# Lower weight parts from an accumulating transfer instead of GpSimd subtractions, in an attention, dense-layer and expert kernel on one core

## The chip, the core and the metric

The kernel runs on one core of a Trainium2 chip. A core has five engines with a queue each, which run side by side: TensorE (PE; its weight loads are listed as PEld), VectorE (DVE), ScalarE (ACT), GpSimd (POOL) and SyncE (SP), which issues transfers. Sixteen DMA engines do the transfers of all queues. The metric is the device time of one execution in microseconds.

## What is computed

```python
def _moe2_ref(x, w_gate, w1, w2):            # after attention and a dense layer
    logits = x @ w_gate                      # 2304 tokens, 8 experts
    order = np.argsort(-logits.flatten())    # greedy: best pair of token and expert first
    ...                                      # an expert takes at most cap = 288 tokens
    for e in range(E):
        mask = assigned == e
        h = np.maximum(x[mask] @ w1[e], 0.0)
        out[mask] = h @ w2[e]
```

Ahead of it, a linear-feature attention and `(x @ w_a) * (x @ w_b) @ w_out` produce x. The result is float32; the kernel reaches that by splitting every operand of a product into an upper part (rounded to the type `F32R`) and a lower part (the rest), and adding three products: upper by upper, upper by lower, lower by upper.

## The kernel before

The program has three stages. Attention and the dense layer run until about 673 us (`Attention`, `Bilinear`). Then a router (`Router`) assigns tokens to experts in seven rounds: in each, VectorE compares and sums small tables, TensorE counts over partitions with many small products, and the two wait for one another. When the first expert is full, its tokens are known and `Experts` starts on it while the router goes on; so router and experts share the engines until about 975 us, and the last experts run alone.

An expert is eight chunks of 128 hidden features. For a chunk, `weights` (L920) gets one tile `raw` of 128 x 1024 float32 (512 KB: 512 columns of w1, 512 of w2), which SyncE loads from HBM (L917), and makes the upper part `wh` and the lower part `wl`. TensorE then does 12 products into `pa` (4 blocks by 3 passes: wh by xl, wh by xh, wl by xh), ScalarE and VectorE make the two parts `hh` and `hl` of the positive part, and 12 more products with the second half of wh and wl add into `po`. The `po` products of a chunk come after the `pa` products of the next one. Around an expert's end, `turn` transposes the next expert's gathered tokens (xg to xh and xl), and `turn_back` transposes results, which GpSimd scatters to the output (`out<-ob`, L902).

What sets the order:
- TensorE's order is written out by hand: `program` interleaves the steps of `Experts.products` with the router's phases by a table of estimated costs. TensorE never reorders, so a late operand stops all that is behind it.
- The other engines' order is set by a scheduler from the dependencies. Each queue runs in order too.
- `raw`, `wh` and `wl` have four buffers each (two pools of two, used in turn). The parts of a chunk can be made once the `po` products of the chunk four before have run; a load can start once the last reader of that `raw` is done.
- GpSimd's queue holds the subtractions of `wl`, the gathers `xg<-yd` (L881) and the scatters, in one order; an expert has three gathers and three scatters, each of 96 rows of 512 float32 (192 KB).

Before the change ScalarE writes `wh` as a rounded copy of `raw` (L924), and GpSimd subtracts it from `raw` in four pieces of 256 columns (L927).

Of the kernel before, what the change touches and what calls it, by code (L numbers as in the profile page):

```python
# [17 lines left out]
AF = mybir.ActivationFunctionType  # L18
OP = mybir.AluOpType
# [43 lines left out]
EARLY = 3  # L63
CUT = 2
SLOTS = 1
PIECE = 256
CNT, AT, ASSIGN, NEXT, TOKENS, COLUMNS, CANDS = 0.4, 0.05, 0.85, 5.6, 4.25, 2.35, 2.1
EAGER = 5
THR16, THR32, SEEN, POP = 0.7, 1.05, 0.12, 1
# [3 lines left out]
def f32(ap):  # L73
    return ap.bitcast(F32)
# [795 lines left out]
class Experts:  # L870
# [47 lines left out]
        return w, raw  # L918

    def weights(self, f):  # L920
        w, raw = self.raws.pop(0) if self.raws else self.load(f)
        wh, wl = [w.tile([128, 1024], F32R, name=n) for n in ("wh", "wl")]

        self.nc.scalar.copy(wh, raw)  # L924
        for c in range(0, 1024, PIECE):
            here = slice(c, c + PIECE)
            self.nc.gpsimd.tensor_tensor(wl[:, here], raw[:, here], f32(wh[:, here]), OP.subtract)  # L927
        return wh, wl

    def outputs(self, i):  # L930
# [273 lines left out]
```

## Time and profile before

| what | us |
|---|---|
| median of three runs | 1062.22 (1055.92 to 1063.88) |
| the profiled execution | 1050.81 |
| its span, first to last instruction | 1049.0 |
| TensorE busy | 966.7 (92%) |
| VectorE busy | 708.2 (68%) |
| ScalarE busy | 380.4 (36%) |
| GpSimd busy | 384.5 (37%) |
| GpSimd subtractions L927, 256 | 182.5 |

Matmuls are pipelined, so a busy TensorE is not one at its peak. The granted clock is a share of 2.4 GHz; 0.5 is 1.2 GHz. Waits are inferred from semaphores: a wait for several is put down to the one that came last. Instructions that issue transfers from SyncE are not counted as busy. "Line" and "L" give the line of the kernel before; behind the edit the lines of the changed kernel are lower by one or two.

### The profile page before, as it was taken

How to read it: one execution, taken by the hardware profiler on the slowest of the kernel's cores; microseconds unless marked ns; L12 is line 12 of the kernel's file. 1: busy time of each engine (PE TensorE's matmuls, PEld its weight loads, DVE VectorE, ACT ScalarE, POOL GpSimd, SP SyncE). 2: the span in 40 equal slices, each digit the busy share in tenths (PEclk: the TensorE clock that was granted, in tenths of full speed). 3: DMA queues.
4: the chain of work that ended last, by engine and by line, in shares of the span. 5: the costliest groups of instructions: out<-in, count | busy, mean ns of one | idle time of the engine just before them, and what ended most of it. 6: DMA issues, size and time to landing. Idle time of an engine off the chain costs nothing.

```text
span 1049.0 us, 18392 instructions
## 1 busy us (share of the span) xinstructions
PE 966.7 (92%) x6683; PEld 895.3 (85%) x6683; DVE 708.2 (68%) x2044; ACT 380.4 (36%) x769; POOL 384.5 (37%) x450
## 2 busy tenths in 40 slices
PE   6868898999999999999999999979987989897996
PEld 5867788989989999999999997768887978887996
DVE  7899999779887656854588886555647474665110
ACT  5755555433333333332211321122423323232452
POOL 3346565323311211210000000155656556556784
PEclk8889999999999999999999999967999989898999
DMA  8366676555443434432722331243243333334451
GB/s 269 109 186 188 209 245 190 217 166 161 141 148 122 134 111 138 122 99 83 268 81 81 111 120 62 81 134 124 75 146 113 117 108 104 121 107 126 131 164 39
DMA packets 66939, 142.98 MB, mean 136 GB/s; under 512 B 6944, under 2 KB 31648, under 8 KB 66720
## 3 DMA queue, kind: packets, MB, share of 16 engines
q1 hardware_dynamic: 63776, 132.36, 39.5%
q0 software_dynamic: 3072, 9.44, 3.1%
q8 instruction: 53, 0.87, 0.3%
q14 instruction: 38, 0.31, 0.1%
HBM read 118.96 MB, written 22.81 MB: 135 GB/s over the span
## 4 chain that ended last, share of the span: by engine, by line
PE 58%; DVE 9%; POOL 2%; issue 2%; DMA 1%; ACT 0%; POOLq 0%; SPq 0%; ACTq 0%; DVEq 0%
PE ab L81 19%; PE pa L81 10%; PE y L81 10%; PE po L81 8%; PE count L690 3%; PE count L823 2%; PE pa L254 2%; POOL wl L927 1%; PE kv L224 1%; PE pa L889 1%; DVE gone L756 1%; DVE pos L793 1%; PE count L688 1%; PE pa L235 1%; DVE scr L497 1%
## 5 line engine op out<-in xcount | busy, mean ns | idle before, releaser
L927 POOL TENSOR_TENSOR wl<-raw,wh 128x256 fp32r<-128x256 f32 x256 | 182.5, 743 | 283.0 <-DMA raw<-in_w 192.5
L81 PE MATMUL ab<-xl,w_hi 128*128 128x384 f32 x576 | 203.8, 354 | 1.5 <-DVE xl L93 1.5
L81 PE MATMUL ab<-xh,w_hi 128*128 128x384 f32 x576 | 195.5, 339 | 0.0
L81 PE MATMUL ab<-xh,w_lo 128*128 128x384 f32 x576 | 195.3, 339 | 0.0
L81 PE MATMUL y<-wo,gh 128*128 128x512 f32 x372 | 119.1, 401 | 1.5 <-ACT gh L92 1.5
L81 PEld LDWEIGHTS ab<-xl,w_hi 128*128 128x128 f32 x576 | 109.4, 190 | 4.6 <-DVE xl L93 1.9
L81 PEld LDWEIGHTS ab<-xh,w_hi 128*128 128x128 f32 x576 | 109.4, 190 | 1.8
L81 PEld LDWEIGHTS ab<-xh,w_lo 128*128 128x128 f32 x576 | 109.0, 189 | 0.0
L924 ACT CAST wh<-raw 128x1024 fp32r<-128x1024 f32 x64 | 67.2, 1050 | 112.0 <-PE po L81 88.6
L81 PE MATMUL pa<-xl,wh 128*128 128x288 f32 x256 | 84.2, 329 | 16.6 <-DVE hl L1001 8.6
L93 POOL TENSOR_TENSOR lo<-raw,hi 128x384 fp32r<-128x384 f32 (+4 forms) x46 | 49.3, 1071 | 126.0 <-ACT hi L92 126.0
L497 DVE SCALAR_TENSOR_TENSOR scr<-ybs,wg 128x512 bf16<-128x512 f32 x120 | 88.4, 737 | 4.3 <-ACT ybs L493 2.4
L81 PE MATMUL pa<-xh,wh 128*128 128x288 f32 x256 | 82.9, 324 | 0.0
L81 PE MATMUL pa<-xh,wl 128*128 128x288 f32 x256 | 82.4, 322 | 0.0
L81 PE MATMUL po<-hh,wl 128*128 128x288 f32 x256 | 81.6, 319 | 0.0
L81 PE MATMUL po<-hh,wh 128*128 128x288 f32 x256 | 80.8, 316 | 0.0
L81 PE MATMUL po<-hl,wh 128*128 128x288 f32 x256 | 80.4, 314 | 0.0
L163 POOL TENSOR_TENSOR tn<-tn 128x384 f32<-128x384 f32 (+4 forms) x43 | 40.1, 932 | 105.2 <-DMA tn<-in_qn 50.4
L81 PEld LDWEIGHTS y<-wo,gh 128*128 128x128 f32 x372 | 65.5, 188 | 9.9 <-issue 1.9
L81 PE MATMUL y<-wo,gl 128*128 128x512 f32 x186 | 73.0, 393 | 0.0
L1000 ACT ACTIVATE hh<-pa 128x288 fp32r<-128x288 f32 x64 | 26.3, 411 | 118.3 <-PE pa L81 116.5
L81 PEld LDWEIGHTS pa<-xl,wh 128*128 128x128 f32 x256 | 52.8, 206 | 18.6 <-DVE hl L1001 13.6
(246 smaller groups left out, 2184.6 us busy)
## 6 DMA issues: line engine op xcount, KB each, us to landing
raw<-in_w SPq DMA_DIRECT2D x64, 512.0 KB, 3.6
wo<-sd SPq DMA_DIRECT2D x38, 512.0 KB, 3.3
wg<-in_wab SPq DMA_DIRECT2D x22, 512.0 KB, 4.0
sd<-wo SPq DMA_DIRECT2D x12, 512.0 KB, 2.9
va<-in_va SPq DMA_DIRECT2D x16, 325.0 KB, 4.1
ybs<-in_wout SPq DMA_DIRECT2D x10, 512.0 KB, 3.9
yd<-ybs SPq DMA_DIRECT2D x18, 256.0 KB, 2.7
xraw<-xd SPq DMA_DIRECT2D x20, 192.0 KB, 2.9
```

The lines of the kernel that those rows point to most:

```text
L81: nc.tensor.matmul(out, lhs[l], rhs[r], start=first and i == 0, stop=last and i == 2)
L93: lo_engine.tensor_tensor(lo, src, f32(hi), OP.subtract)
L163: nc.gpsimd.tensor_tensor(tn, tn, tn, OP.mult)
L224: nc.tensor.matmul(kv[:, j], f[:, j], vals[b, p][:, vt, j], start=(ends[0] and k == 0 and j == 0), stop=(ends[1] and k == len(todo) - 1 an ...
L235: nc.tensor.transpose(pt[:, c:c + 128], ph[:, k, j], self.ident)
L254: nc.tensor.matmul(nv[:, i, j], qt[:, j], self.kvs[b, p][:, j], start=True, stop=True)
L497: self.nc.vector.scalar_tensor_tensor(self.scr, rows, 1.0, self.wg[:, e], op0=OP.mult, op1=OP.mult, accum_out=total)
L690: nc.tensor.matmul(cnt, cmp[:, c], oh[:, :, c], start=False, stop=(c == NT - 1))
L823: nc.tensor.matmul(got[:CH, :2 * NCH], slot[:, :, c], ids2[:, c].rearrange("p i j -> p (i j)"), start=(c == 0), stop=(c == NT - 1))
L924: self.nc.scalar.copy(wh, raw)
L927: self.nc.gpsimd.tensor_tensor(wl[:, here], raw[:, here], f32(wh[:, here]), OP.subtract)
L1000: nc.scalar.activation(hh, ps[:, :CAP], AF.Relu)
```

## The change

```diff
-PIECE = 256
...
     def weights(self, f):
         w, raw = self.raws.pop(0) if self.raws else self.load(f)
         wh, wl = [w.tile([128, 1024], F32R, name=n) for n in ("wh", "wl")]
-
+        self.nc.scalar.activation(wl, raw, AF.Copy, scale=-1.0)
+        self.nc.gpsimd.dma_start(wl, raw, accum_op=OP.add)
         self.nc.scalar.copy(wh, raw)
-        for c in range(0, 1024, PIECE):
-            here = slice(c, c + PIECE)
-            self.nc.gpsimd.tensor_tensor(wl[:, here], raw[:, here], f32(wh[:, here]), OP.subtract)
         return wh, wl
```

ScalarE now first writes the negated rounded copy into `wl`. A transfer that GpSimd's queue issues then adds `raw` to `wl` in place: raw minus its upper part is the lower part. Then ScalarE writes `wh` as before. `wl` is whole at once when the transfer has landed, where it came in four pieces. The order on TensorE and on SyncE is the same as before.

GpSimd's queue at the start of the experts and through the second one, before (wl is the lower part, xg a gather of tokens, out a scatter of results):

```order
L927 TENSOR_TENSOR wl<-raw,wh 128x256 x4
L881 DMA xg<-yd,ids 96x512 x3
L927 TENSOR_TENSOR wl<-raw,wh 128x256 x28
L881 DMA xg<-yd,ids 96x512 x3
L927 TENSOR_TENSOR wl<-raw,wh 128x256 x19
L902 DMA out<-ob,ids 2304x512
```

And the same place in the changed kernel:

```order
L925 DMA wl<-raw 128x1024
L880 DMA xg<-yd,ids 96x512 x3
L925 DMA wl<-raw 128x1024 x7
L880 DMA xg<-yd,ids 96x512 x3
L925 DMA wl<-raw 128x1024 x5
L901 DMA out<-ob,ids 2304x512
```

Four subtractions of a chunk have become one transfer at the same place of the queue.

ScalarE's queue where an expert ends and the next one's tokens are turned, before (wh is the upper part of a chunk, xh that of the tokens, ot a result, hh the upper part of a hidden block):

```order
L924 CAST wh<-raw 128x1024
L891 CAST xh_11074<-pa 128x288
L891 CAST xh_11107<-pa 128x288
L956 COPY ot_11211<-po_10470 128x288
L891 CAST xh_11126<-pa 128x288
L956 COPY ot_11213<-po_10471 128x288
L891 CAST xh_11138<-pa 128x288
L956 COPY ot_11215<-po_10472 128x288
L956 COPY ot_11217<-po_10473 128x288
L924 CAST wh<-raw 128x1024
L1000 ACTIVATE hh<-pa 128x288 x2
```

And the same place in the changed kernel:

```order
L924 ACTIVATE wl<-raw 128x1024
L890 CAST xh_10994<-pa 128x288
L890 CAST xh_11027<-pa 128x288
L955 COPY ot_11129<-po_10404 128x288
L926 CAST wh<-raw 128x1024
L890 CAST xh_11046<-pa 128x288
L890 CAST xh_11058<-pa 128x288
L955 COPY ot_11131<-po_10405 128x288
L955 COPY ot_11133<-po_10406 128x288
L955 COPY ot_11135<-po_10407 128x288
L924 ACTIVATE wl<-raw 128x1024
L926 CAST wh<-raw 128x1024
```

The negation stands where the copy wh stood, and the copy has moved down between the second and the third xh.

## Rows read from the trace of the kernel before

**Rows 1.** Stretches: from, to, length, busy us and instructions per engine, clock, DMA share, GB/s.

```profile
693.00:975.00 282.00, 253.82 (x2213) 234.19 (x2212) 160.65 (x599) 87.61 (x150) 165.25 (x220) 0.90 0.37 112
975.00:1040.00 65.00, 63.51 (x484) 62.69 (x484) 11.55 (x26) 32.43 (x59) 50.34 (x70) 1.00 0.40 122
```

**Rows 2.** TensorE's waits, 690 to 975 us: total us, times, longest us.

```profile
PE pa L81 <- DVE hl L1001: 8.6, 3, 4.6
PE pa L81 <- DVE total L795: 7.5, 2, 3.8
PE count L823 <- DVE ids L814: 7.1, 3, 4.0
PE count L803 <- DVE total L795: 1.8, 1, 1.8
```

**Rows 3.** Timeline around 806 to 811 us: start, duration, engine, line, instruction, idle before.

```profile
806.77 2.83 POOL L927 TENSOR_TENSOR wl<-raw,wh 128x256 fp32r<-128x256 f32 x4
806.90 2.73 DVE L756 TENSOR_TENSOR gone<-gone,new 128x18 f32<-128x18 f32 x1
...
811.06 0.40 PE L81 MATMUL pa<-xl,wh 128*128 128x288 f32 x1 [4.65 <-DVE hl L1001]
```

**Rows 4.** Three VectorE lines of the router: shortest/median/longest ns.

```profile
L756 DVE TENSOR_TENSOR gone<-gone,new x7: 170/706/2740, 672.7 to 942.6; 128x18 f32<-128x18 f32 x7
...
L725 DVE TENSOR_SCALAR over<-best,at x7: 235/776/786, 668.3 to 937.6; 128x18 bf16<-128x18 f32 x7
...
L755 DVE TENSOR_REDUCE new<-run x7: 396/414/424, 672.3 to 942.2; 128x18 f32<-128x144 bf16 x7
```

**Rows 5.** The page's costliest groups: count, busy us, mean ns, idle before.

```profile
L927 POOL TENSOR_TENSOR wl<-raw,wh 128x256 fp32r<-128x256 f32 x256 | 182.5, 743 | 283.0 <-DMA raw<-in_w 192.5
...
L924 ACT CAST wh<-raw 128x1024 fp32r<-128x1024 f32 x64 | 67.2, 1050 | 112.0 <-PE po L81 88.6
```

**Rows 6.** Stretches behind six stalls: the two ends of the clock, and the sum.

```profile
811.06:815.00 3.94, 3.94 (x18) 3.79 (x19) 3.84 (x16) 0.41 (x1) 0.38 (x1) 0.58 0.69 215
...
955.70:958.40 2.70, 2.70 (x12) 2.65 (x13) 0.31 (x2) 0.01 (x1) 1.74 (x2) 0.50 0.16 30
...
sum 26.05, PE 26.05 PEld 25.41 DVE 18.13 ACT 1.84 POOL 9.76; mean PE 4.34 PEld 4.24 DVE 3.02 ACT 0.31 POOL 1.63
```

**Rows 7.** Timeline around 753 us: VectorE beside a scatter that GpSimd issues.

```profile
753.00 0.78 DVE L725 TENSOR_SCALAR over<-best,at 128x18 bf16<-128x18 f32 x1
...
753.82 0.31 DVE L727 TENSOR_TENSOR gq<-oh,over 128x288 bf16<-128x288 bf16 x1
753.90 1.04 POOL L902 DMA_INDIRECT out<-ob,ids  x1 [0.16 <-issue]
...
754.16 0.45 DVE L731 TENSOR_REDUCE rows<-gq 128x16 bf16<-128x288 bf16 x1
```

**Rows 8.** Timeline at an expert boundary: TensorE's wait before a transposition.

```profile
788.11 0.44 PE L889 MATMUL pa<-ident,xg 96*128 96x96 f32 x3 [0.72 <-DVE xl L892]
```

**Rows 9.** Transfers: KB each and us to landing; stretches with one load, and one scatter.

```profile
raw<-in_w SPq DMA_DIRECT2D x64, 512.0 KB, 3.6
...
wg<-in_wgate SPq DMA_DIRECT2D x1, 2048.0 KB, 7.4
...
xg<-yd,ids POOLq DMA_INDIRECT x24, 3.1
...
994.40:996.75 2.35, 2.35 (x21) 2.34 (x20) 0.43 (x1) 1.19 (x2) 2.17 (x4) 1.00 0.71 223
...
997.10:998.10 1.00, 1.00 (x10) 1.00 (x9) 0.12 (x1) 0.41 (x1) 1.00 (x3) 1.00 0.67 197
```

**Rows 10.** Timeline: a chunk's cast on ScalarE and TensorE's first product with its wl.

```profile
780.51 1.05 ACT L924 CAST wh<-raw 128x1024 fp32r<-128x1024 f32 x1 [2.11 <-PE po L81]
...
792.85 0.29 PE L81 MATMUL pa<-xh,wl 128*128 128x288 f32 x1
...
995.56 1.05 ACT L924 CAST wh<-raw 128x1024 fp32r<-128x1024 f32 x1 [1.23 <-PE po L81]
...
1002.95 0.29 PE L81 MATMUL pa<-xh,wl 128*128 128x288 f32 x1
...
1027.95 1.05 ACT L924 CAST wh<-raw 128x1024 fp32r<-128x1024 f32 x1 [1.22 <-PE po L81]
```

## Prediction

> **What bounds the kernel now.** I start with the busy time by stretch, since the change touches only the last third. Up to 673 us the program runs attention and the dense layer, where no line of the diff runs. From 693 to 975 us the router and the experts share the engines, and from 975 to 1040 us the last experts run alone [rows 1]. In the second stretch TensorE is busy 253.8 of 282 us at a mean clock of 0.90; in the third 63.5 of 65 at 1.00. So the tail is TensorE's own work, and the stretch with the router has two leaks: 28 us of idle time and a clock that falls.
>
> The waits of TensorE say who ends the idle time: hl (8.6 us), total (7.5 and 1.8) and ids (7.1), 25.0 us together, all of them VectorE results [rows 2]. No wait for a weight chunk stands among them. The timeline shows why VectorE is late. At 806.90 us the sum gone, 128x18, takes 2.73 us; its quickest run takes 0.17 [rows 3, 4]. At 806.77 GpSimd had begun four subtractions that take 2.83 us together, and the sum ends with them. TensorE then stands still for 4.65 us until hl, which is queued behind gone on VectorE, arrives at 811.06 [rows 3]. It is not that instruction alone: over, with a minimum of 235 ns, has a median of 776, about one subtraction (743 ns) longer [rows 4, 5]. A reduction in the same chain, new, stays between 396 and 424 ns throughout [rows 4]. So certain VectorE instructions wait for GpSimd's subtractions. The reader is to see that GpSimd's 182.5 us [rows 5] are not on TensorE's path as work, but as a brake on VectorE.
>
> After each long stall the clock is at the lower of its two levels, 1.2 GHz. I took the six stretches behind the stalls of over 2.5 us (behind the last two stalls, from after the count products), up to where the clock is back: 26.05 us in all, with a granted clock between 0.50 and 0.58 [rows 6].
>
> **The change, part by part.** TensorE's order and SyncE's stay as they are.
>
> Removed: 256 subtractions, 182.5 us of GpSimd. Worth nothing on GpSimd itself; it frees VectorE. The longest stalls follow stretched instructions: gone alone gives 2.73 - 0.17 = 2.56 of the 4.65 us, and the rest comes in steps of about half a microsecond like that of over, of which the same round has several. I take all 25.0 us of [rows 2]. With the stalls goes the low clock behind them: 26.05 us at about 0.52 would be some 13.5 us at full clock, so 12.5 us saved. Term: **-37.5 us**.
>
> Does an issue of a transfer brake VectorE as a subtraction does? At 753.90 GpSimd issues a scatter for 1.04 us; under it gq takes 0.31 us and the reduction rows 0.45, while over, which ran under subtractions just before, took 0.78 [rows 7]. So no. The Trainium skill (SBUF — State Buffer, "Who interferes with whom") puts it so: a VectorE instruction with two SBUF inputs contends with a GpSimd instruction that reads SBUF. The same page ("SBUF: two separate sides") warns that VectorE's two-port modes keep GpSimd from writing descriptors; by that the issues would be late by the length of such an instruction. The scatter in these rows took 1.04 us beside VectorE; by the page's warning the issues would be later, which is one way into the same-time rival.
>
> Added on ScalarE: 64 negations of 128x1024. The copy of that shape takes 1050 ns [rows 5], so 67 us. ScalarE is busy 32.4 of 65 us in the tail [rows 1]; 17 more leave a quarter free, so it hides behind TensorE. Two consequences do not hide by themselves. The transfer starts 1.05 us after the buffers are free: below. And at each expert boundary the copy wh now stands between the second and the third xh on ScalarE. TensorE already waits there (0.72 us at 788.11, on xl, which follows xh) [rows 8]. Up to 1.05 us more at seven boundaries would be 7; I take **+5 us**.
>
> Added on GpSimd's queue: 64 accumulating transfers of 512 KB. No row of before has one. Its time on the sixteen DMA engines, X, decides, so I bound it by the nearest rows. A plain load of 512 KB keeps the engines busy 0.71 of 2.35 us = 1.67 us, start-up included [rows 9]. Without start-up: 2048 KB land in 7.4 us and 512 KB in 3.6, so 1536 KB more cost 3.8 us, or 1.27 us for 512 KB [rows 9]. The transfer must fetch two operands, raw and wl, and write one. Bounds: one pass at 1.27 us below; three passes one after the other at 1.67 = 5.0 above. I take two at the streaming price, **X = 2.54 us**, as both operands lie in SBUF and only the fetching doubles. The Trainium skill (Collectives: The Full Stack, "The bandwidth ceiling: the fold count and why AG ≠ RS ≠ AR") says that an adding transfer runs at about half the rate of a copy because it reads two sources on one ring. That speaks against the change, compared with one pass: by one pass the tail term below is nothing, by two it is 8 us. No row of before shows an adding transfer.
>
> Latency: a gather of 192 KB lands 3.1 us after issue [rows 9]; minus its bytes (192 KB at 404 KB per us, 0.5) plus 2.54 gives 5.2 us, and with the negation 6.3, or 8.0 when one load is ahead of it. What is there to cover it? A chunk's buffers come free four chunks ahead: the cast at 780.51 fills what TensorE first needs, as wl, at 792.85, so 12.3 us; in the tail 995.56 to 1002.95, 7.4 us [rows 10]. With the router running the transfer is hidden with 4 to 6 us to spare; without this cover each chunk would pay what is beyond it. In the tail it is about even.
>
> Throughput: per chunk a load 1.67, the accumulate 2.54, and three gathers and three scatters an expert, 6 x 0.67 / 8 = 0.50 [rows 9], 4.71 us in all. In the tail the casts from 995.56 to 1027.95 are nine chunks apart, 3.60 us each [rows 10]; 61 us of tail at that pace are 17 of the 64 chunks, so 47 lie in the stretch with the router. There TensorE would need (282 - 32.5) / 47 = 5.3 us a chunk: the DMA engines keep up. In the last 12 loads they don't: 12 x (4.71 - 3.60) = 13.3 us, less some 5 us of lead from the stretch before. Term: **+8 us**.
>
> Sum: -37.5 + 5 + 8 = -24.5 us. The profiled execution took 1050.81 us (span 1049.0 and 1.8 around it), 11.4 below the median of the runs, 1062.22, and below all three. Counted from its own time the sum gives 1026; the runs are judged by their median, so I give 1062.2 - 24.5 = **1038 us**.
>
> **Rivals.**
> One pass. The accumulate costs what a copy costs, X = 1.27, and the tail stays at 3.60 us a chunk: 1062.2 - 32.5 = 1030. For it: nothing in the rows but the lower bound.
> Same time. Two passes at the load's own price, X = 3.34. With the router: 47 x (5.51 - 5.3) = 10 us; tail: 12 x (5.51 - 3.60) - 5 = 18. The gain of 32.5 shrinks to about 5: 1057. Late issues would work the same way. For it: 1.67 is what a load was seen to take; against: a part of that is start-up at the memory, and this transfer reads SBUF.
> Slower: the DMA engines become the bound of all experts. One mechanism, one price: X above 3.4 us, where 47 x (2.17 + X - 5.3) + 12 x (2.17 + X - 3.60) - 5 exceeds 32.5. Three passes at 1.27 (3.8 us) give 1085, at 1.67 (5.0 us) 1155. TensorE would then wait for wl in every chunk. For it: no row shows the adding path at speed. Against: the engines are only 0.37 to 0.40 busy now [rows 1].
>
> **How the numbers follow.** Forecast 0.42, one pass 0.15, same time 0.18, slower 0.25. A measurement of this kernel tells about 1% (10.6 us) from no change. Faster by more: forecast, one pass and a little of the third case, 0.60; within 1%: 0.15; slower: 0.25. The range reaches from a little under the one-pass time, 1022, to the mildest of the slower case, 1085; left out are the dearer transfers, about 0.2. The likeliest case alone: 1030 to 1050.
>
> **What would show it.** The median of gone at 0.18 us and of over at 0.24, no stall of TensorE over 2 us between 693 and 975 us, and a mean clock there near 0.97. In the tail chunks of 4 to 4.7 us with waits of TensorE on wl. A DMA share of about 0.85 with the router running; if it is at 0.95 and TensorE waits for wl from the first expert on, X is over 3.4 and the forecast is wrong. If gone is still slow, the brake was something else.

## Result and profile after

The changed kernel takes 1031.7 us (1028.1 to 1035.1, four runs) against 1059.6 for the kernel before on the same chip: a ratio of 0.9735, with a 95% interval from 0.9677 to 0.9793. A second measurement, beside the experiments, gave 0.9774 [0.9740, 0.9807]. The forecast was 1038 in a range from 1022 to 1085, faster with 0.60; 1031.7 lies in that range. The profiled execution has a span of 1026.3 us, 22.7 less than that of before.

To compare kernels I cut every trace at four instants that all of them have: the start of `hl` of the first chunk (number 0), the start of `hl` of chunk 47 (the router ends there), the end of the last `po` product, and the end. Between the first two, router and experts share the engines; between the second and third the last experts run alone. TensorE executes the same products in each stretch in every kernel.

The stretches of the kernel before, cut so: from, to, length, then busy us and instructions of PE, PEld, DVE, ACT and POOL, the granted clock, the DMA share, GB/s.

```profile
698.75:978.54 279.79, 251.87 (x2198) 232.96 (x2199) 158.71 (x592) 87.86 (x148) 163.55 (x217) 0.91 0.36 111
978.54:1039.09 60.55, 59.14 (x455) 58.60 (x453) 11.34 (x25) 30.46 (x55) 47.28 (x66) 1.00 0.41 124
1039.09:1049.00 9.91, 1.80 (x12) 1.01 (x10) 0.00 (x0) 2.08 (x5) 2.75 (x3) 0.74 0.21 60
```

The same three stretches of the changed kernel:

```profile
700.68:944.52 243.84, 242.82 (x2199) 225.38 (x2200) 122.55 (x591) 130.11 (x194) 77.08 (x82) 0.95 0.94 227
944.52:1013.93 69.41, 61.39 (x455) 58.78 (x453) 11.32 (x25) 42.95 (x69) 18.09 (x21) 1.00 0.93 229
1013.93:1026.30 12.37, 1.80 (x12) 1.01 (x10) 0.00 (x0) 2.08 (x5) 2.85 (x3) 0.73 0.17 49
```

The first stretch is 35.95 us shorter. TensorE's idle time in it fell from 27.9 us (279.79 - 251.87) to 1.0, and its busy time by 9.05 for the same products, as the clock rose from 0.91 to 0.95. VectorE needs 122.55 us in place of 158.71 for the same 591 or 592 instructions: 36.2 us of VectorE's busy time had been brake, not work. The second stretch is 8.86 us longer: TensorE does the same 455 matrix instructions and stands idle 8.0 us where it stood 1.4. The end is 2.5 us longer, and the first stretch starts 1.9 us later. Together -35.95 + 8.86 + 2.46 + 1.93 = -22.7.

TensorE's waits in the two stretches of the changed kernel (total us, times, longest; the first row is of the tail, the other two of the stretch with the router), which answer to [rows 2]:

```profile
PE pa L80 <- DMA wl<-raw: 6.8, 7, 1.7
...
PE pa L80 <- DVE xl L891: 0.6, 3, 0.2
PE pa L888 <- DVE xl L891: 0.3, 1, 0.3
```

The waits for hl, total and ids have gone. The three VectorE lines of [rows 4], in the changed kernel (shortest/median/longest ns):

```profile
L755 DVE TENSOR_TENSOR gone<-gone,new x7: 170/178/195, 673.8 to 915.9; 128x18 f32<-128x18 f32 x7
...
L724 DVE TENSOR_SCALAR over<-best,at x7: 235/236/238, 669.4 to 911.8; 128x18 bf16<-128x18 f32 x7
...
L754 DVE TENSOR_REDUCE new<-run x7: 418/427/441, 673.3 to 915.4; 128x18 f32<-128x144 bf16 x7
```

Gone (170 to 195 ns) and over (235 to 238) now stay close to their shortest times of before, 170 and 235; new, which was never braked, is much as it was (median 427 ns, before 414).

The page's groups of the two new operations of the changed kernel (count, busy us, mean ns, idle before), and its two largest DMA queues (packets, MB, share of 16 engines' span); in the kernel before, q0 had 3072 packets and 3.1%:

```profile
q1 hardware_dynamic: 63776, 132.36, 39.9%
q0 software_dynamic: 12288, 43.00, 20.8%
...
L924 ACT ACTIVATE wl<-raw 128x1024 fp32r<-128x1024 f32 x64 | 68.1, 1065 | 80.9 <-PE po L80 59.2
...
L925 POOL DMA_DIRECT2D wl<-raw x64 | 57.3, 913 | 377.8 <-DMA raw<-in_w 192.9
```

From q0 follows what one accumulating transfer costs the sixteen engines: (20.8% of 1026.3 - 3.1% of 1049.0) / 64 = 2.83 us.

The tail, in the timeline of the changed kernel: one chunk's transfer is issued at 963.74, and TensorE, which wants its wl first at 971.17, waits for it until 972.92. The negation of a later chunk has itself waited for a load.

```profile
963.74 0.89 POOL L925 DMA_DIRECT2D wl<-raw  x1 [1.44 <-ACT wl L924]
...
971.50 1.06 ACT L924 ACTIVATE wl<-raw 128x1024 fp32r<-128x1024 f32 x1 [2.00 <-DMA raw<-in_w]
...
972.92 0.40 PE L80 MATMUL pa<-xh,wl 128*128 128x288 f32 x1 [1.75 <-DMA wl<-raw]
```

From issue to use that is 9.2 us, and the negation comes ahead of it; [rows 10] gave 7.4 us of cover in the tail. Loads and accumulating transfers wait for the same sixteen engines, which are busy 0.93 of this stretch.

### The profile page after: what moved, and what is told of

It is laid out like the page before. It is cut to its first block, busy times and chain, and to the rows that moved or that the text cites. A ratio compares the mean times of both kernels' runs of the same rounds, so it can differ in the third digit from the quotient of the medians.

```text
span 1026.3 us, 18252 instructions
## 1 busy us (share of the span) xinstructions
PE 961.3 (94%) x6683; PEld 889.6 (87%) x6683; DVE 671.7 (65%) x2044; ACT 439.7 (43%) x833; POOL 264.4 (26%) x258
## 3 DMA queue, kind: packets, MB, share of 16 engines
q1 hardware_dynamic: 63776, 132.36, 39.9%
q0 software_dynamic: 12288, 43.00, 20.8%
## 4 chain that ended last, share of the span: by engine, by line
PE 57%; DMA 5%; issue 5%; DVE 2%; POOL 1%; ACT 1%; POOLq 0%; SPq 0%; ACTq 0%; DVEq 0%
PE ab L80 20%; PE y L80 10%; PE pa L80 10%; PE po L80 7%; DMA wl<-raw 3%; PE count L689 2%; PE count L822 2%; PE pa L253 2%; DMA raw<-in_w 1%; PE kv L223 1%; POOL wl L925 1%; PE pa L898 1%; PE pa L234 1%; PE count L687 1%; DVE scr L496 1%
## 5 line engine op out<-in xcount | busy, mean ns | idle before, releaser
L925 POOL DMA_DIRECT2D wl<-raw x64 | 57.3, 913 | 377.8 <-DMA raw<-in_w 192.9
L924 ACT ACTIVATE wl<-raw 128x1024 fp32r<-128x1024 f32 x64 | 68.1, 1065 | 80.9 <-PE po L80 59.2
L80 PE MATMUL pa<-xh,wh 128*128 128x288 f32 x256 | 80.7, 315 | 0.0
L1000 DVE SCALAR_TENSOR_TENSOR hl<-pa,hh 128x288 fp32r<-128x288 f32 x64 | 29.1, 454 | 64.2 <-ACT hh L999 52.9
L424 ACT COPY gv<-ab 128x384 f32<-128x384 f32 x72 | 34.4, 478 | 77.1 <-PE ab L80 77.0
```

Of the source, the lines that this page charges most:

```text
L80: nc.tensor.matmul(out, lhs[l], rhs[r], start=first and i == 0, stop=last and i == 2)
L424: nc.scalar.copy(gv, ps)
L924: self.nc.scalar.activation(wl, raw, AF.Copy, scale=-1.0)
L925: self.nc.gpsimd.dma_start(wl, raw, accum_op=OP.add)
L1000: nc.vector.scalar_tensor_tensor(hl, ps[:, :CAP], 0.0, f32(hh), op0=OP.max, op1=OP.subtract)
```

## Experiments

The theory: the gain is VectorE freed from the brake that GpSimd's subtractions put on it, and the price is DMA-engine time, which counts only where TensorE uses up weights faster than the engines can load and accumulate them, in the tail. The rivals on the gain's side: it comes from GpSimd's queue (a shorter queue issues gathers, scatters and transfers earlier). On the price's side: it is a fixed delay of the new transfer, or ScalarE's added negations.

All kernels, cut at the same four instants (us; where an experiment adds lines of code, the line numbers of its rows are higher by a few; VectorE's busy time is that of the first stretch; behind the runs' median its ratio to the kernel before on the same chip, whose median was between 1050.2 and 1059.6 us in the four measurements):

| kernel | hl 0 to hl 47 | VectorE busy | to the last po | to the end | median | ratio |
|---|---|---|---|---|---|---|
| before | 279.79 | 158.7 | 60.55 | 9.91 | 1059.6 | 1 |
| changed | 243.84 | 122.6 | 69.41 | 12.37 | 1031.7 | 0.9735 |
| changed, again | 243.48 | 122.5 | 70.36 | 12.35 | 1031.1 | 0.9774 |
| scratch subtractions | 278.85 | 157.3 | 74.93 | 12.36 | 1071.3 | 1.0133 |
| four fills | 252.71 | 132.8 | 71.86 | 12.43 | 1044.1 | 0.9905 |
| six fills | 316.88 | 132.9 | 86.63 | 12.45 | 1121.2 | 1.0583 |
| one whole subtraction | 283.46 | 155.9 | 60.61 | 9.83 | 1054.6 | 1.0010 |
| no transfer | 244.90 | 122.4 | 60.30 | 9.84 | 1025.5 | 0.9672 |
| half transfer | 245.50 | 122.5 | 60.92 | 12.33 | 1025.0 | 0.9677 |
| plain copy | 243.43 | 122.6 | 61.69 | 15.14 | 1024.8 | 0.9747 |
| transfer and a half | 336.87 | 123.4 | 114.59 | 10.56 | 1167.1 | 1.1086 |
| hybrid | 244.44 | 122.5 | 60.50 | 11.65 | 1020.0 | 0.9671 |

**The subtractions put back, for nothing.** The changed kernel with the old work of GpSimd beside the new.

```diff
         self.nc.scalar.copy(wh, raw)
+        spare = w.tile([128, 256], F32, name="spare", bufs=1)
+        for c in range(0, 1024, 256):
+            here = slice(c, c + 256)
+            self.nc.gpsimd.tensor_tensor(spare, raw[:, here], f32(wh[:, here]), OP.subtract)
```

> The changed kernel, and beside it the old four GpSimd subtractions of 128x256 a chunk, into a scratch tile that nobody reads. Theory, two-operand subtractions on GpSimd brake VectorE: gone goes back from 0.18 to 0.5 to 2.7 us in several rounds, over to about 0.78, TensorE stalls for 20 to 30 us on VectorE results and its clock drops behind them; the DMA cost of the changed kernel stays, so 1058 to 1072 us, no faster than before. Rival, the gain came from GpSimd's queue being free for gathers and scatters, not from VectorE: also slower, 1045 to 1060, but gone and over stay at 0.18 and 0.24. Second rival, the gain came from elsewhere (wl and wh made earlier or in another order): 1030 to 1036.

Measured: 1071.28 us, ratio 1.0133 [1.008, 1.0185] to the kernel before. The stretch with the router, then TensorE's waits in it, then gone, in this kernel:

```profile
703.16:982.01 278.85, 253.59 (x2198) 233.81 (x2199) 157.25 (x592) 130.54 (x194) 214.86 (x266) 0.91 0.85 202
...
PE count L822 <- DVE ids L813: 11.3, 6, 4.0
PE pa L80 <- DVE total L794: 5.0, 2, 2.5
PE pa L80 <- DVE hl L1004: 3.6, 4, 2.5
...
L755 DVE TENSOR_TENSOR gone<-gone,new x7: 165/702/778, 676.7 to 946.4; 128x18 f32<-128x18 f32 x7
```

The whole gain is gone: the stretch is within 1 us of that of before, VectorE within 1.5, the clock at 0.91 again, and TensorE waits for no transfer in it. Against the changed kernel the stretch loses 35.0 us and the tail 5.5. Of the expected signs one failed: over's median stayed at 0.23 us (its longest was 1.26), so another set of instructions was hit than in the kernel before.

**GpSimd busy without reading.** The same place, with fills that read nothing; first six a chunk, then four.

```diff
         self.nc.scalar.copy(wh, raw)
+        spare = w.tile([128, 512], F32, name="spare", bufs=1)
+        for _ in range(6):        # four_fills: range(4)
+            self.nc.gpsimd.memset(spare, 0.0)
```

> The changed kernel, and beside it six GpSimd fills of a scratch tile (128x512) a chunk, which read nothing and take about as long as the four subtractions did, some 3 us a chunk. Theory, the brake is in the reading of operands from SBUF: gone stays at 0.18 us and over at 0.24, time 1029 to 1036. Rival, GpSimd's occupied queue is what cost the time (late gathers, scatters and issues): 1045 to 1060, as with the subtractions. Second rival, any GpSimd work on SBUF brakes VectorE, writing too: gone and over as slow as in the kernel before, 1055 to 1070.

> The changed kernel with four GpSimd fills of a scratch tile (128x512) a chunk in place of six. Six took 4.9 us a chunk (0.82 each), which with the issues is more than a chunk of the tail lasts; four take 3.3 us, as much as the four scratch subtractions did (3.4). Theory, VectorE is braked by GpSimd's reading: TensorE's stalls on VectorE results stay under 10 us and gone at 0.18; what is lost is late issues of the transfers (TensorE waits on wl), 1035 to 1055 us. Rival, GpSimd's occupied queue accounts for the loss with the subtractions too: as much as with them, 1065 to 1075, with waits on wl in the stretch with the router. Second rival, fills brake VectorE as subtractions do: stretched instructions of VectorE sum to over 25 us (38 with the scratch subtractions), 1060 to 1075.

Measured: 1121.2 us with six, 1044.14 with four (ratio 0.9905 [0.9876, 0.9933] to the kernel before). One fill lasts about 0.82 us in the rows, but the next begins some 0.47 us after it, so the two overlap: six in a row take 3.2 us, about what was meant, and not the 4.9 us that the second expectation adds up. But they stand unevenly in GpSimd's queue, up to 13 in a row (6.92 us), so that the transfer behind them is issued late. TensorE waits for wl with the router running already, and since that loss is mixed with the brake's, six settle little (that run of fills and the issue behind it, and the wait in the first stretch of the six):

```profile
791.63 6.92 POOL L929 MEMSET spare<- 128x512 f32 x13
798.25 1.12 POOL L925 DMA_DIRECT2D wl<-raw  x1
...
PE pa L80 <- DMA wl<-raw: 41.3, 13, 7.2
```

Four settle more. Their stretch with the router, then gone and the two lines of over, then the longest over beside the fills that ran:

```profile
704.80:957.51 252.71, 244.86 (x2199) 226.38 (x2200) 132.84 (x592) 130.26 (x194) 163.54 (x263) 0.95 0.91 217
...
L755 DVE TENSOR_TENSOR gone<-gone,new x7: 161/170/179, 679.2 to 929.1; 128x18 f32<-128x18 f32 x7
...
L723 DVE TENSOR_SCALAR over<-best,at x7: 243/245/3508, 674.6 to 921.7; 128x18 bf16<-128x18 f32 x7
L724 DVE TENSOR_SCALAR over<-best,at x7: 234/236/3373, 674.8 to 921.9; 128x18 bf16<-128x18 f32 x7
...
921.55 3.65 POOL L929 MEMSET spare<- 128x512 f32 x7
...
921.73 3.51 DVE L723 TENSOR_SCALAR over<-best,at 128x18 bf16<-128x18 f32 x1
```

GpSimd is busy 163.54 us here and 163.55 in the kernel before, in a stretch of the same work; yet the stretch is 252.71 and not 279.79. So an occupied GpSimd queue is not what cost the 36 us. But my theory, that only reading brakes, fell as well: the fills cost VectorE 10.3 us (132.84 - 122.55) and the stretch 8.9. They hit another set of instructions: over (one input from SBUF) was held up to 3.5 us, to the end of seven fills in a row, while gone (two inputs) was never touched. The other stretched lines were of over's kind (TENSOR_SCALAR) or stood queued behind one. The Trainium skill (SBUF — State Buffer, "Who interferes with whom") has both: an instruction with two SBUF inputs contends only with a GpSimd instruction that reads, and certain one-input forms, among them tensor_scalar, can take both ports and are then blocked by any GpSimd work; the rows agree.

**One subtraction of 1024 columns.** The kernel before, with its subtractions whole.

```diff
-PIECE = 256
+PIECE = 1024
```

> The kernel before with one subtraction of 1024 columns a chunk in place of four of 256. If a braked VectorE instruction waits for the end of the running GpSimd instruction: over goes from a median of 0.78 us up to 1.5 to 2.8, gone stays at 2.7 at most, TensorE's stalls on VectorE grow from 25 to 35 to 50 us, time 1070 to 1090. If the brake is only a shared rate: over and gone as before, time 1052 to 1064.

Measured: 1054.64 us, ratio 1.001 [0.9981, 1.004]. Both expectations were half right: over waits longer, as the first said (1.24 us in the median), and the time stays, as the second said. Three VectorE lines of this kernel:

```profile
L756 DVE TENSOR_TENSOR gone<-gone,new x7: 161/167/181, 677.4 to 952.3; 128x18 f32<-128x18 f32 x7
...
L724 DVE TENSOR_SCALAR over<-best,at x7: 244/1241/1570, 672.8 to 946.7; 128x18 bf16<-128x18 f32 x7
...
L757 DVE TENSOR_TENSOR given<-given,run x7: 215/1820/2231, 677.5 to 952.1; 128x144 bf16<-128x144 bf16 x7
```

A single instruction (given, over) waits longer than in the kernel before, up to 2.23 us where a whole subtraction takes 2.39, and others (gone) escape; in sum VectorE is busy 155.9 us where it was 158.7. In these two profiles the cut into pieces moves the brake and hardly changes its sum.

**The transfer taken away, halved, made a copy.** Three kernels on what the tail pays for.

```diff
-        self.nc.gpsimd.dma_start(wl, raw, accum_op=OP.add)
                                                              # no_accum: nothing in its place
+        self.nc.gpsimd.dma_start(wl[:, :512], raw[:, :512], accum_op=OP.add)   # half_accum
+        self.nc.gpsimd.dma_start(wl, raw.bitcast(F32R))                        # copy_instead
```

> The changed kernel (1031.7 us) without the accumulating transfer; the lower parts of the experts' weights are therefore missing from the sum. Throughput theory: the transfers cost time only in the tail, where the DMA engines are the limit; the stretch with the router (from chunk 0's first product to chunk 47's, 246.6 us in the changed kernel's profile) stays within 3 us, the tail from chunk 47's first product to the last po product shrinks from 71.7 to 62 or 63 us, and the time is 1020 to 1024 us. Rival, the DMA engines (0.95 busy) hold up the stretch with the router too: that stretch shrinks by 5 to 10 us more and the time is 1010 to 1017. Second rival, the accumulates cost nothing and the long tail comes from ScalarE's negations, which are kept here: 1030 to 1033.

> The changed kernel with the accumulating transfer cut to the first 512 of 1024 columns (the lower parts of the w2 half are missing from the result). Throughput theory: the transfer takes 1.4 us of the DMA engines in place of 2.8, so a chunk asks for 1.67 + 1.4 + 0.5 = 3.6 us, as much as TensorE needs in the tail: the tail's loss goes nearly whole, 71.7 to 63 or 64 us, time 1021 to 1025. Rival, a fixed delay from issue to landing is what makes TensorE wait in the tail: about half of the loss or more stays, tail 67 to 71 us, time 1026 to 1032.

> The accumulating transfer replaced by a plain copy of raw into wl, of the same size, from the same queue (the lower parts of the experts' weights are therefore wrong). Two-pass step of the prediction, adding makes a transfer fetch two operands and so doubles it: the copy takes 1.3 to 1.5 us of the DMA engines in place of 2.83, so queue q0 has a share of 11 to 13% in place of 20.8, a chunk asks for 3.6 us, the tail is 60.5 to 62 us as with the half transfer, time 1022 to 1027. Rival, any transfer of 512 KB within SBUF from this queue costs 2.8 us and the adding is free: share 20 to 21%, tail 68 to 71, time 1029 to 1034.

(The expectations count the tail from chunk 47's first product, 2.3 us ahead of its hl.) Measured: 1025.49 (a little above the 1020 to 1024 expected), 1024.97 and 1024.81 us; the ratios to the kernel before are 0.9672 [0.9618, 0.9726], 0.9677 [0.9630, 0.9724] and 0.9747 [0.9717, 0.9778]. The two stretches without the transfer, and then with half of it:

```profile
708.76:953.66 244.90, 242.88 (x2199) 225.26 (x2198) 122.43 (x591) 129.78 (x194) 34.17 (x36) 0.94 0.42 127
953.66:1013.96 60.30, 59.52 (x455) 58.68 (x453) 11.29 (x25) 42.27 (x69) 5.54 (x6) 1.00 0.38 116
```

```profile
705.25:950.75 245.50, 243.67 (x2199) 225.95 (x2200) 122.51 (x591) 129.89 (x194) 76.97 (x82) 0.94 0.71 175
950.75:1011.67 60.92, 59.95 (x455) 58.75 (x453) 11.29 (x25) 42.49 (x69) 18.04 (x21) 1.00 0.75 180
```

The DMA engines go from a share of 0.94 to 0.42 and the stretch with the router does not shrink at all: there the transfer is free. In the tail half a transfer is as good as none (60.9 and 60.3 us), which a fixed delay would not allow, and the negations, still there in both, cost nothing. The medians show less than the stretches: 9.1 us of the tail and 2.5 of the end make 11.6, the medians differ by 6. In these two profiles hl 0 came at 708.8 and 705.3 us, 5 to 8 later than in the changed kernel's, after the same instructions; whether that is chance or not I did not settle.

The plain copy's q0:

```profile
q0 software_dynamic: 12288, 43.00, 12.8%
```

(12.8% of 1020.9 - 32.5) / 64 = 1.53 us for a copy, against 2.83 for the same bytes added: 1.85 times. The loads' queue q1 took 414 us of the engines in the kernel before (39.5% of 1049.0) and 409 in the changed one (39.9% of 1026.3), so such shares did not grow with the load, and the two prices can be compared. The adding costs, not the queue or the size. The copy's tail is 61.7 us, as with half a transfer. Its whole time shows less of that: its end is 15.1 us long, 2.8 more than in the changed kernel, and its ratio is no better than the changed kernel's two.

**Half a transfer more.** Where does the room end?

```diff
         self.nc.gpsimd.dma_start(wl, raw, accum_op=OP.add)
+        self.nc.gpsimd.dma_start(wl[:, :512], raw[:, :512], accum_op=OP.add)
```

> The changed kernel with a second accumulating transfer of 512 of the 1024 columns behind the first (the lower parts of the w1 half are therefore wrong). By the half and the whole transfer it adds 1.5 us of the DMA engines, 4.3 a chunk, so that a chunk asks for 1.67 + 4.3 + 0.5 = 6.5 us where TensorE needs 5.2 with the router running and 3.6 alone. Theory, the limit is the DMA engines' throughput and the changed kernel stands just below it (5.0 against 5.2): the stretch from hl 0 to hl 47 grows from 244 by 47 x 1.3 = 61 us, the tail from 69 to 95 to 110, time 1105 to 1145. Rival, the measured busy share of 0.95 overstates the load and there is room yet: stretch 244 to 255, tail 75 to 85, time 1040 to 1065.

Measured: 1167.09 us, ratio 1.1086 [1.1051, 1.1121], beyond what the theory gave. The first stretch, TensorE's wait in it, the tail, q0, and GpSimd's wait at the second transfer of a chunk (both stretches):

```profile
705.58:1042.45 336.87, 278.73 (x2199) 254.83 (x2200) 123.43 (x592) 130.90 (x194) 116.93 (x128) 0.81 0.91 201
...
PE pa L80 <- DMA wl<-raw: 57.6, 24, 5.6
...
1042.45:1157.04 114.59, 72.51 (x455) 69.65 (x453) 11.31 (x25) 43.06 (x69) 33.21 (x37) 0.82 0.84 180
...
q0 software_dynamic: 21504, 59.78, 27.6%
...
POOL wl L926 <- DMA wl<-raw: 228.5, 54, 8.7
```

The transfers cost (27.6% of 1167.6 - 32.5) / 64 = 4.53 us a chunk; with a load of 1.67 and 0.50 for gathers and scatters that is 6.7. The tail runs close to that, 114.59 / 17 = 6.74 us a chunk; with the router it is 336.87 / 47 = 7.17. So TensorE does wait for wl all along, as in the slower rival of the prediction, and its clock falls to 0.81 and 0.82. But the run does not show that the DMA engines alone set this pace. The second transfer adds to what the first has written, so it is issued when the first has landed: 54 times GpSimd's queue stood still for it, 228.5 us in all, and the gathers and scatters behind it with it. In the tail the DMA engines were busy 0.84, less than the 0.93 of the changed kernel. How much of the loss is the engines' time and how much this waiting in line was not separated.

**The hybrid.** If the transfer is free while the router runs and only costs in the tail, and the subtractions cost only while the router runs, each should do its part: the transfer for the first 49 chunks, whose parts are made before the router is done, the old subtractions for the last 15.

```diff
-        self.loaded, self.raws, self.clock = 0, [], 0.0
+        self.made, self.loaded, self.raws, self.clock = 0, 0, [], 0.0
...
+        late = self.made >= 49
+        self.made += 1
+        if not late:
             self.nc.scalar.activation(wl, raw, AF.Copy, scale=-1.0)
             self.nc.gpsimd.dma_start(wl, raw, accum_op=OP.add)
         self.nc.scalar.copy(wh, raw)
+        for c in range(0, 1024 * late, 256):
+            here = slice(c, c + 256)
+            self.nc.gpsimd.tensor_tensor(wl[:, here], raw[:, here], f32(wh[:, here]), OP.subtract)
```

> The accumulating transfer for the first 49 chunks, whose parts are made while the router runs, and the old GpSimd subtractions for the last 15. Throughput theory: the stretch from chunk 0's hl to chunk 47's hl stays at 244 to 246 us, as in the changed kernel and without the transfer, since VectorE is unbraked for as long as the router needs it; the tail from there to the last po product goes from 69.4 to 60.5 or 61 us, and the time is 1020 to 1025 us, below the changed kernel by 7 to 11. Rival, the subtractions brake hl and xl on VectorE in the tail as they did the router: tail 65 to 70, time 1027 to 1033.

> The changed kernel once more, beside the hybrid: 1029 to 1035 us by every theory; it gives the hybrid's distance on the same chip.

Measured on one chip: 1019.96 us (1016.9 to 1022.7, six runs) against 1031.14 (1029.1 to 1034.3) for the changed kernel; to the kernel before 0.9671 [0.9638, 0.9704]. The hybrid's two stretches:

```profile
700.41:944.85 244.44, 243.41 (x2198) 225.57 (x2199) 122.46 (x591) 129.14 (x193) 76.94 (x83) 0.95 0.94 227
944.85:1005.35 60.50, 59.13 (x455) 58.59 (x453) 11.34 (x25) 30.47 (x55) 46.76 (x65) 1.00 0.44 132
```

The first is the changed kernel's, the second that of before. 11.2 us below the changed kernel, it beats both. VectorE's 25 instructions of the tail take 11.34 us beside the subtractions and 11.32 without: no brake on these.

## Why the prediction was right, step by step

- **The brake.** The reading that GpSimd's subtractions hold VectorE up, and TensorE behind it, was right: taken away, VectorE saves 36.2 us of busy time; put back for nothing, the scratch subtractions return 34.7 of them. The idle time that went with it was forecast at 25.0 us and measured at 26.9. One reading beside it was off: the median of over, 776 ns, is 541 ns above its shortest 235, and so shorter by a quarter than one subtraction (743 ns), not about one longer; nothing in the sum rests on it.
- **The clock.** Forecast -12.5, measured -9.05 (TensorE's busy time for the same products). The term was too big because not every low stretch came from a stall: in the changed kernel the clock still falls seven times, each time after the 18 narrow products of count, with no idle time ahead. The products in the timeline, and the stretches before and after the fall:

```profile
759.63 3.28 PE L822 MATMUL count<-ids,slot 128*96 128x6 bf16 x18
...
759.80:763.00 3.20, 3.20 (x21) 3.20 (x20) 0.05 (x1) 1.23 (x2) 0.89 (x1) 1.00 1.02 219
763.70:767.10 3.40, 3.40 (x16) 3.40 (x16) 0.46 (x1) 0.78 (x2) 2.76 (x3) 0.50 1.05 254
```

  The seven stretches are 3.4 us each at 1.2 GHz, 23.8 us that no freed VectorE removes. Two of the six stretches that I counted stood behind count products, and I put them down to the stall ahead of them. Hence also a mean clock of 0.94 to 0.95 with the router, where I had said about 0.97.
- **The expert boundary.** Forecast +5, measured nothing: TensorE's waits on xl add up to 0.9 us in the whole stretch. The copy stands between the second and the third xh on ScalarE as the order showed, and TensorE does not wait for it; what covers it I did not test. This and the clock's term are the two that were mis-sized, in opposite directions: the stretch with the router was forecast at -32.5 and came out at -35.95.
- **The price of the transfer.** X was taken as 2.54 us and measured at 2.83; the copy, taken as 1.27, is 1.53. The step that chose two passes between the ends of 1.27 and 5.0 was right, by the measured factor of 1.85. The Trainium skill (Collectives: The Full Stack, "The bandwidth ceiling: the fold count and why AG ≠ RS ≠ AR") gives about half the rate for a reduce-scatter against an all-gather between cores, because the add reads two sources; the factor measured here within one core agrees with it.
- **Hidden with the router, paid in the tail.** With X = 2.83 a chunk asks the DMA engines for 1.67 + 2.83 + 0.50 = 5.0 us. The stretch with the router gives it 243.84 / 47 = 5.19: hidden, as said, at a share of 0.94 instead of the 0.85 forecast, and with only 0.2 us to spare. In the tail it is over 3.60, and TensorE waits for wl: +8.86 against a forecast of +8. That the two agree is partly luck: with the true X the formula, 12 x (5.0 - 3.60) - 5, gives 11.8; by that formula the lead from the stretch before was 8 us and not 5, which no run checks. The sign that was to refute the forecast, a share of 0.95 with waits for wl from the first expert on, came only in its first half: the share was 0.94, but TensorE waited for no wl before the tail.
- **What was left out.** The end after the last product is 2.5 us longer, and the start 1.9 us later. These 4.4 us nearly cancel the 5 us of the expert boundary that did not come: by luck the sum came out closer to the profiles than its terms.
- **The rivals.** One pass is excluded by X. Same time needed 3.34 and slower over 3.4 us: X stayed below both. Late issues did not show either: the 64 issues took 0.91 us each, less than the scatter's 1.04 in [rows 7]. The run with 4.53 shows the slower rival's sign, waits for wl all along, and a dearer time than its formula: 1062.2 - 32.5 + 47 x (2.17 + 4.53 - 5.3) + 12 x (2.17 + 4.53 - 3.60) - 5 = 1128, where the run took 1167. The formula has neither the lower clock nor a second transfer that waits for the first.

The sum was -24.5 us; the profiles give -22.7, the medians of the runs -27.9. The profiled execution of before was itself 8.8 us below its median of 1059.6, that of after 3.6 below its own.

## What to carry to other kernels

An engine off the critical path can still set the pace, through what it does to its neighbour: look for an instruction of one shape whose longest time is many times its shortest, and for what ran beside it at those moments. Work moved to the DMA engines is free as long as the sum of their times per step stays below the time of the step, and that has to be worked out for each stage: here 5.0 us was free against 5.2 and cost 9 us against 3.6. Where two ways of doing a thing cost in different stages, use each where it is free.

## What was not expected of the hardware

- GpSimd fills, which read nothing, also hold VectorE up: over, 0.24 us, took up to 3.5 us beside seven fills in a row, and gone, which subtractions had stretched to 2.7, was untouched.
- TensorE's clock falls to 1.2 GHz after 18 narrow products (128x6, 3.3 us) though TensorE never stood still, and stays there for 3.4 us.
- The time from the last product to the end is 9.8 to 9.9 us without the new transfers, 12.3 to 12.5 with 64 of them, 11.65 in the hybrid, 15.1 with copies, and 10.6 with 128 transfers. I found no cause that fits all five; it stays open.
